# Where the left half of an output leaves from: fp16 tiles and the GpSimd queue in place of fp32 tiles and the sync queue

## The chip, the cores and the metric

The kernel runs on one core of a Trainium2 chip. The metric is device time in microseconds. The engines named below are PE (TensorE), DVE (VectorE), ACT (ScalarE), POOL (GpSimd) and SP (SyncE). POOL and SP compute little or nothing in the part that matters here: they issue DMAs.

## The reference

A dilated sliding-window attention feeds a layer of "soft MoE" slots. Only the end of the second part is touched by the change.

```python
def _moe_ref(x, phi, w1, w2):            # x: attention output, 4608 x 512
    logits = x @ phi                     # 4608 x 32
    d = softmax(logits over rows)        # dispatch
    slot_input = (d.T @ x).reshape(8, 4, 512)
    for e in range(8):
        h = np.maximum(slot_input[e] @ w1[e], 0.0)   # 4 x 1024
        slot_out[e] = h @ w2[e]                      # 4 x 512
    slot_out = slot_out.reshape(32, 512)
    c = softmax(logits over slots)       # combine
    return (c @ slot_out).astype(np.float32)         # 4608 x 512, 9.44 MB
```

Every one of the 4608 output rows depends on all of `slot_out`, so no output can be stored before the second weight matrix of all eight experts has been read.

## The kernel before

The first 137 us of the program are the attention, the logits and the slot inputs. All inputs are read by DMAs that POOL issues and that cast fp32 in HBM to fp16 on chip. The last of these are the second weights `w2`. The last two experts, 6 and 7 (`HALVED`), are loaded as column halves: first the left 256 columns of both, then the right 256 columns (`load_w2(e, half)`, L232).

The rest is an order written out by hand under `manual_schedule`: each engine runs its instructions in the order of the program text.

- `slot_out(half, experts)` multiplies the hidden rows by `w2` for one column half (PE, L681). After the last expert of a half, ACT copies that half of `slot_out` to SBUF as `so_sb` (L689).
- `combine(half, pair)` makes 256 rows by 256 columns of the output: two matmuls (L697) into a PSUM tile `f`, of which there are four, then a scaled copy to an SBUF tile `ot0` (left half) or `ot1` (right half), by ACT in two instructions for an even pair (L709) and by DVE in one for an odd pair (L713), and one DMA to `out` (L719). Left halves are fp32 tiles stored by SP; there are six buffers for the eight of them. Right halves are fp16 tiles stored by POOL, with a cast to fp32 on the way, and have eight buffers.
- `combine_full(pair)` makes 256 whole rows: one matmul for each 128 rows (L730), the first evicted by ACT (L732) and the second by DVE (L736) into one fp16 tile `of` of seven buffers, and one casting DMA by POOL (L743).

The order around the change is this:

```python
        slot_out(0, HALVED)
        at = {5: 0}
        for pair in range(NSPLIT // 2):          # 8 left halves, pairs 0 to 7
            combine(0, pair)
            if pair in at:
                slot_out(1, (HALVED[at[pair]],))  # expert 6, right columns
        slot_out(1, HALVED[1:])                   # expert 7, right columns
        for pair in range(NSPLIT // 2, NFIN // 2):
            combine_full(pair)                    # pairs 8 to 17, whole rows
            if pair >= NFIN // 2 - NSPLIT // 2:
                combine(1, pair - (NFIN // 2 - NSPLIT // 2))
```

So the left halves of the first eight pairs are made while the last right-hand weights are still arriving; then come whole rows, and from pair 10 on each is followed by the right half of an early pair.

Each DMA on POOL's queue signals one of eight semaphores in turn, and its issue waits until the DMA eight places before it has landed.

Of the kernel before, what the change touches and what calls it, by code (L numbers as in the profile page):

```python
# [9 lines left out]
FP32 = mybir.dt.float32  # L10
FP16 = mybir.dt.float16
# [13 lines left out]
DMODEL = H * D  # L25
# [18 lines left out]
NH = DMODEL // 2  # L44
NSPLIT = 16
# [25 lines left out]
def kernel(  # L71
# [10 lines left out]
    nc = tc.nc  # L82
# [534 lines left out]
    out_pool = tc.alloc_tile_pool(name="outp", bufs=1)  # L617
# [75 lines left out]
    def combine(half, pair):  # L693
        fp = psum_f.tile([128, 2, NH], FP32, name=f"f{half}_{pair}", tag="f")
        r0 = 256 * pair
        for k in range(2):
            nc.tensor.matmul(  # L697
                fp[:, k, :],
                ET[:, r0 + 128 * k : r0 + 128 * k + 128],
                so_sb[:, NH * half : NH * half + NH],  # L700
                start=True,
                stop=True,
                skip_group_check=True,
            )
        ot = out_pool.tile([128, 2, NH], (FP32, FP16)[half], name=f"ot{half}_{pair}", tag=f"ot{half}", bufs=6 + 2 * half)
        if pair % 2 == 0:
            for k in range(2):
                blk = 2 * pair + k
                nc.scalar.activation(  # L709
                    out=ot[:, k, :], in_=fp[:, k, :], func=AF.Copy, scale=rrow[:, blk : blk + 1]  # L710
                )
        else:
            nc.vector.tensor_tensor(  # L713
                out=ot,
                in0=fp,
                in1=rrow[:, 2 * pair : 2 * pair + 2, None].broadcast_to([128, 2, NH]),
                op=ALU.mult,
            )
        (nc.sync, nc.gpsimd)[half].dma_start(  # L719
            out=out[r0 : r0 + 256, NH * half : NH * half + NH].rearrange("(k p) n -> p k n", k=2),  # L720
            in_=ot,
        )

    def combine_full(pair):
        r0 = 256 * pair
        ot = out_pool.tile([128, 2, DMODEL], FP16, name=f"of_{pair}", tag="of", bufs=7)
        for k in range(2):
            blk = 2 * pair + k
            fp = psum_f.tile([128, DMODEL], FP32, name=f"f_{blk}", tag="f")
            nc.tensor.matmul(fp, ET[:, 128 * blk : 128 * blk + 128], so_sb, start=True, stop=True)  # L730
            if k == 0:
                nc.scalar.activation(  # L732
                    out=ot[:, k, :], in_=fp, func=AF.Copy, scale=rrow[:, blk : blk + 1]
                )
            else:
                nc.vector.tensor_scalar(  # L736
                    out=ot[:, k, :],
                    in0=fp,
                    scalar1=rrow[:, blk : blk + 1],
                    scalar2=None,  # L740
                    op0=ALU.mult,
                )
        nc.gpsimd.dma_start(  # L743
            out=out[r0 : r0 + 256, :].rearrange("(k p) n -> p k n", k=2), in_=ot
        )

    with tc.manual_schedule(engines=None):
        slot_out(0, ORDER[:6])
        slot_out(1, ORDER[:6])
        slot_out(0, HALVED)  # L750
        at = {5: 0}
        for pair in range(NSPLIT // 2):
            combine(0, pair)
            if pair in at:
                slot_out(1, (HALVED[at[pair]],))
        slot_out(1, HALVED[1:])
        for pair in range(NSPLIT // 2, NFIN // 2):
            combine_full(pair)
            if pair >= NFIN // 2 - NSPLIT // 2:
                combine(1, pair - (NFIN // 2 - NSPLIT // 2))  # L760
# [36 lines left out]
```

The softmax here doesn't subtract the row's maximum and nothing guards it: scores larger than these inputs give would overflow.

## Time and profile before

| | us |
|---|---|
| median of three runs (lowest, highest) | 185.91 (185.76, 186.13) |
| the profiled execution, its own time | 185.91 |
| its span, first to last instruction | 184.1 |
| last expert-7 matmul of the left half starts (L681) | 151.71 |
| SP issues the first left half (L719) | 154.13 |
| last `w2` lands, last right-half matmuls start (L681) | 157.15 |
| POOL issues the first whole-row tile (L743) | 161.36 |
| POOL issues its last output DMA (L719) | 174.32 |

Positions in the table are microseconds from the start of the span. The profiled execution's time is 1.8 us above its span, and it equals the median. In the views, a DMA "share" above 1 means that engines hold more than one packet at a time, and GB/s counts bytes as they are written: a weight load counts its fp16 bytes, an output store its fp32 bytes.

### The profile page before, as it was taken

The numbers are of one execution on the slowest core, as the hardware profiler recorded it, in microseconds if no ns is written. First come the engines' busy times: TensorE is split into PE (matmuls) and PEld (weight loads), VectorE is DVE, ScalarE is ACT, GpSimd is POOL, SyncE is SP. The second block draws the span as 40 slices with busy tenths as digits, with TensorE's granted clock in tenths as the row PEclk, the third lists the DMA queues.
The fourth block names the chain that finished last, engine by engine and source line by source line (L and its number), as shares of the span: only waits on it lengthen the run. The fifth ranks groups of instructions, "written<-read, shape, count | busy, mean of one in ns | idle before, by whom it ended". The sixth has DMA issues, their size and how long they took to land.

```text
span 184.1 us, 5522 instructions
## 1 busy us (share of the span) xinstructions
PE 142.3 (77%) x2448; PEld 85.5 (46%) x2448; DVE 104.8 (57%) x225; ACT 90.0 (49%) x161; POOL 75.1 (41%) x104
## 2 busy tenths in 40 slices
PE   3157989999999999999999999998782278587000
PEld 0134556466467467467467467564431144232000
DVE  2687779849849849849859754540420004399000
ACT  2053458576567676576576576551020006588000
POOL 7743654454453454453623755111111100089800
PEclk9999999999999999999999999965589556789755
DMA  5999999999999999999999999999999999999994
GB/s 88 199 204 212 202 206 208 210 207 206 214 209 203 212 210 203 213 206 206 213 207 208 209 211 216 214 215 214 214 214 212 197 196 191 319 325 405 408 410 91
DMA packets 32023, 41.00 MB, mean 223 GB/s; under 512 B 2144, under 2 KB 19680, under 8 KB 32000
## 3 DMA queue, kind: packets, MB, share of 16 engines
q0 software_dynamic: 29536, 38.44, 112.6%
q1 hardware_dynamic: 2464, 2.22, 3.7%
q8 instruction: 19, 0.31, 0.6%
q14 instruction: 4, 0.03, 0.0%
HBM read 62.18 MB, written 9.44 MB: 389 GB/s over the span
## 4 chain that ended last, share of the span: by engine, by line
DMA 42%; PE 30%; ACT 8%; issue 6%; POOL 6%; DVE 3%; POOLq 0%; DVEq 0%; ACTq 0%
DMA w<-in_moe_w_dram 27%; DMA vs<-in_v_dram 7%; DMA raw<-in_q_dram 6%; PE lg L413 5%; PE o_p L344 4%; PE sa L287 4%; ACT p L298 4%; PE sa L276 3%; PE sb L276 3%; ACT ot L709 3%; DMA out_dram<-ot 2%; PE f L730 2%; PE u L455 1%; PE rd L394 1%; PE vb L188 1%
## 5 line engine op out<-in xcount | busy, mean ns | idle before, releaser
L298 ACT ACTIVATE p<-sa 128x960 f16<-128x960 f32 (+2 forms) x24 | 21.4, 891 | 29.4 <-PE sb L287 28.6
L344 PEld LDWEIGHTS <-p 128*128 128x128 f16 (+2 forms) x544 | 19.4, 98 | 12.6 <-issue 8.6
L241 DVE STREAM_TRANSPOSE qk<-raw 128x576 uint32<-128x576 uint32 x16 | 20.0, 1251 | 5.7 <-DMA raw<-in_q_dram 4.5
L250 DVE STREAM_TRANSPOSE qk<-raw 128x320 uint32<-128x320 uint32 (+1 forms) x32 | 21.5, 675 | 0.3
L298 ACT ACTIVATE p<-sb 128x960 f16<-128x960 f32 (+2 forms) x24 | 21.2, 884 | 0.0
L287 PE MATMUL sa<-qk 32*128 32x160 f16 (+4 forms) x416 | 15.7, 212 | 4.0 <-DVE qk L241 4.0
L216 POOL COPY v<-v 32x1024 f16<-32x1024 f16 x8 | 8.3, 1034 | 24.7 <-DVE v L209 24.7
L413 PE MATMUL lg<-xTd,phi 128*128 128x288 f16 x32 | 18.3, 659 | 0.0
L287 PEld LDWEIGHTS <-qk 32*128 32x128 f16 x832 | 11.9, 96 | 13.4 <-issue 8.2
L232 POOL DMA_DIRECT2D w<-in_moe_w_dram x8 | 5.9, 742 | 28.0 <-DMA w<-in_moe_w_dram 23.6
L276 PE MATMUL sa<-masks,ident 128*128 128x480 f16 (+2 forms) x48 | 13.8, 372 | 4.5 <-DMA ident<-ident_d 3.0
L344 PE MATMUL o_p<-v,p 128*128 128x65 f16 (+1 forms) x288 | 16.2, 201 | 0.7 <-ACT v L197 0.7
L713 DVE TENSOR_TENSOR ot<-f,rrow 128x512 f32<-128x512 f32 (+1 forms) x8 | 5.5, 688 | 18.6 <-PE f L697 15.5
L276 PEld LDWEIGHTS <-ident 128*128 128x128 f16 x96 | 8.9, 102 | 15.2 <-issue 8.4
L287 PE MATMUL sb<-qk 32*128 32x160 f16 (+4 forms) x416 | 15.7, 212 | 0.0
L366 DVE TENSOR_TENSOR xp<-o_p,rc_p 128x448 f16<-128x448 f32 (+1 forms) x24 | 14.5, 602 | 0.8
L366 DVE TENSOR_TENSOR xd<-o_d,rc_d 128x448 f16<-128x448 f32 (+1 forms) x24 | 14.5, 602 | 0.8
L681 PE MATMUL so<-w,hTm 128*32 128x256 f16 x128 | 7.2, 361 | 9.3 <-DMA w<-in_moe_w_dram 8.5
L276 PE MATMUL sb<-masks,ident 128*128 128x480 f16 (+2 forms) x48 | 14.0, 372 | 0.4 <-ACT p L298 0.2
L220 POOL DMA_DIRECT2D w<-in_moe_w_dram x16 | 11.4, 713 | 6.3 <-DMA raw<-in_k_dram 2.6
L743 POOL DMA_DIRECT2D out_dram<-of x10 | 7.0, 701 | 15.1 <-ACT of L732 14.0
L188 PE MATMUL va<-vs,orders 32*128 32x256 f16 (+1 forms) x96 | 12.1, 289 | 1.0 <-ACT p L298 1.0
(86 smaller groups left out, 267.2 us busy)
## 6 DMA issues: line engine op xcount, KB each, us to landing
w<-in_moe_w_dram POOLq DMA_DIRECT2D x16, 512.0 KB, 17.0
w<-in_moe_w_dram POOLq DMA_DIRECT2D x6, 1024.0 KB, 27.9
out_dram<-of POOLq DMA_DIRECT2D x10, 512.0 KB, 5.6
vs<-in_v_dram POOLq DMA_DIRECT2D x8, 512.0 KB, 13.6
raw<-in_q_dram POOLq DMA_DIRECT2D x7, 576.0 KB, 15.7
raw<-in_k_dram POOLq DMA_DIRECT2D x7, 576.0 KB, 16.1
w<-in_moe_w_dram POOLq DMA_DIRECT2D x8, 256.0 KB, 24.0
out_dram<-ot SPq DMA_DIRECT2D x8, 256.0 KB, 4.0
```

The costliest lines, as they stand in the source:

```text
L188: nc.tensor.matmul(o.rearrange("p (h d) -> p h d", h=4), l, st[:, 0:4, D * r : D * r + D], start=(r == 0), stop=(r == DIL - 1), skip_group ...
L216: nc.gpsimd.tensor_copy(out=vL[b % NV][0:32, :, :, 0:D], in_=vD[b % NV][96:128, :, :, 0:D])
L220: nc.gpsimd.dma_start(out=w1t[e][:, 2 * i : 2 * i + 2, :], in_=src[:, 2 * i : 2 * i + 2, :])
L241: nc.vector.transpose(out=dst, in_=src)
L250: nc.vector.transpose(out=o, in_=i)
L276: nc.tensor.matmul(sps[h // 2][:, h % 2, 0:n], ident, bias[g], start=True, stop=False, skip_group_check=True,)
L287: nc.tensor.matmul(sps[h // 2][:, h % 2, c0 : c0 + w], kt_[32 * h : 32 * h + 32, k0 : k0 + 128, tt], qt_[32 * h : 32 * h + 32, q0 : q0 + w ...
L298: nc.scalar.activation(out=pt, in_=sps[ab][:, :, 0:n], func=AF.Exp, scale=SCALE)
L344: nc.tensor.matmul(o[p0 : p0 + np_, n, :], l, rr, start=(k == 0), stop=(k == len(jobs) - 1), skip_group_check=True,)
L366: nc.vector.tensor_tensor(out=x.rearrange("p t (h d) -> p (t h) d", h=4)[0:nq, u0:u1, :], in0=o[0:nq, 0:n, 0:D], in1=rc[0:nq, 0:n, None].b ...
L413: nc.tensor.matmul(lp, phi4[:, kc].rearrange("p c s -> p (c s)"), rhs, start=(kc == 0), stop=(kc == 3))
L681: nc.tensor.matmul(so[half][32 * a : 32 * a + 32, :], hTm[2 * g + c // 4][:, c % 4, 32 * j : 32 * j + 32], w2t[e][:, c, NH * half : NH * h ...
```

## The change

Three edits. The left-half tile `ot0` becomes fp16 with eight buffers in place of fp32 with six (`NSPLIT // 2` is 8; `ot1` already had eight). The left-half store goes by POOL's queue in place of SP's, and casts to fp32 on the way. The whole-row tile `of` has eight buffers in place of seven, for ten tiles. The order of right halves between whole rows is the same in both versions.

```diff
-        ot = out_pool.tile([128, 2, NH], (FP32, FP16)[half], name=f"ot{half}_{pair}", tag=f"ot{half}", bufs=6 + 2 * half)
+        ot = out_pool.tile([128, 2, NH], FP16, name=f"ot{half}_{pair}", tag=f"ot{half}", bufs=NSPLIT // 2)
...
-        (nc.sync, nc.gpsimd)[half].dma_start(
+        nc.gpsimd.dma_start(
             out=out[r0 : r0 + 256, NH * half : NH * half + NH].rearrange("(k p) n -> p k n", k=2),
             in_=ot,
         )
...
     def combine_full(pair):
-        ot = out_pool.tile([128, 2, DMODEL], FP16, name=f"of_{pair}", tag="of", bufs=7)
+        ot = out_pool.tile([128, 2, DMODEL], FP16, name=f"of_{pair}", tag="of", bufs=8)
```

The instructions of PE, DVE and ACT are the same in both, in the same order; eight DMA issues move from SP to POOL, ahead of POOL's first L743.

## The prediction, made before the changed kernel was run

> **What bounds the kernel now.** I read the slices of the span first: the DMA engines are busy from start to end.
>
> ```profile
> DMA  5999999999999999999999999999999999999994
> GB/s 88 199 204 212 202 206 208 210 207 206 214 209 203 212 210 203 213 206 206 213 207 208 209 211 216 214 215 214 214 214 212 197 196 191 319 325 405 408 410 91
> ```
>
> About 200 is a full rate while inputs come in (fp16 bytes counted, twice as many read); about 408 is the full rate of outputs. So this is a DMA-bound kernel, and only slices 34 and 35 (156 to 166 us) fall short: 319 and 325 of 408. The change can gain only there. I cut that stretch by events; the last two columns are DMA share and GB/s.
>
> ```profile
> 155.25:158.25 3.00, 1.59 (x21) 0.73 (x21) 0.69 (x1) 0.91 (x4) 0.00 (x0) 0.94 1.03 326
> 158.25:158.50 0.25, 0.00 (x0) 0.00 (x0) 0.00 (x0) 0.25 (x2) 0.00 (x0) 1.00 0.21 74
> 158.50:161.50 3.00, 2.50 (x6) 0.86 (x6) 2.04 (x3) 1.99 (x5) 0.14 (x1) 0.58 1.03 346
> 161.50:162.50 1.00, 1.00 (x5) 0.58 (x4) 0.90 (x2) 0.83 (x2) 0.86 (x2) 0.55 0.22 74
> 162.50:162.75 0.25, 0.25 (x4) 0.13 (x2) 0.00 (x1) 0.25 (x2) 0.25 (x1) 1.00 0.55 172
> 162.75:171.00 8.25, 5.69 (x27) 2.26 (x24) 7.44 (x11) 6.83 (x14) 8.13 (x13) 1.00 1.59 409
> ```
>
> SP's fp32 stores move 326 to 346 GB/s, then there is a hole of a full microsecond before POOL's casting stores begin, and those run at 409 to the end (180.6). Why is there a hole? The chain of waits and the list of waits say what was late:
>
> ```profile
> 154.13 3.60 DMA out_dram<-ot
> ...
> 157.84 0.84 ACT ot L709 x2
> 158.68 0.27 ACT so_sb L689
> ...
> 159.00 2.72 PE f L730 x6
> ```
>
> ```profile
> DVE ot L713 <- DMA out_dram<-ot: 3.0, 1, 3.0
> ACT ot L709 <- DMA out_dram<-ot: 2.1, 1, 2.1
> ```
>
> The seventh left tile needs the buffer of the first, whose store has to land. ACT is held 2.1 us, and behind it in ACT's order stands the copy of the right half of `so_sb`, without which no whole row can start. The timeline has the queues:
>
> ```profile
> 154.13 6.00 SPq L719 DMA_DIRECT2D out_dram<-ot  x8
> 157.15 0.29 PE L681 MATMUL so<-w,hTm 128*32 128x256 f16 x4 [0.60 <-DMA w<-in_moe_w_dram]
> 161.36 2.38 POOL L743 DMA_DIRECT2D out_dram<-of  x3 [14.02 <-ACT of L732]
> 163.73 0.71 POOL L719 DMA_DIRECT2D out_dram<-ot  x1
> ```
>
> POOL sits idle for 14 us before 161.36, so its queue has room.
>
> **What the Trainium skill says.** "DMA: Bandwidth & Descriptors", section "SWDGE vs HWDGE vs iDMA": a cast during a DMA can only be issued from GpSimd. The trace agrees as far as it goes: all fp16-to-fp32 stores are POOL's. The same page, "Latency and other measured facts", gives a first byte after about 0.6 us on the sync path and 1 us on the GpSimd path; here SP's first issue (154.13) to the first stores (155.0, where the rate jumps) is 0.9 us, POOL's (161.36 to 162.55) 1.2 us, and I use the trace. The same page, "Queues, rings and completion order": each DMA engine takes descriptors of one ring in order and alternates between rings, so on an engine that still has weights left, a POOL store stands behind them where an SP store did not. "SBUF — State Buffer", "SBUF: two separate sides": some DVE modes lock GpSimd out while it writes descriptors. The trace shows no such effect: the POOL issues of L719 and L743 take 0.70 to 0.71 us each while DVE writes fp16 tiles from PSUM, and that is the DVE form the left halves take on.
>
> **The change, part by part.** Positions are in the profiled execution, whose own time (185.91, span 184.1) is the median of the runs, so differences carry over unscaled.
>
> 1. Evictions in fp16 instead of fp32: L709 takes 0.42 us either way (2.49/6 in fp32, 0.84/2 in fp16), L713 0.69 and 0.68. Nothing, either way.
>
> 2. Eight buffers for eight left tiles. Matmuls of pairs 6 and 7 ended at about 156.3, so ACT evicts pair 6 by about 157.1 instead of 158.68. Next late is the last weight: PE's last four matmuls start at 157.15 and take 0.29. The `so_sb` copy then starts at 157.5 instead of 158.57, 1.07 us earlier, and L730 and the evictions with it. Tile `of_8` was complete at 160.86 (DVE 160.04 plus 0.82); now 159.8. DVE's 3.0 us wait goes too; nothing but its own L736 stood behind it.
>
> 3. Eight issues leave SP, where nothing stands behind them, and enter POOL ahead of L743. Price 0.71 us each, the row of the right halves, which have the same form. The first is ready when ACT ends at 154.12. A POOL issue that finds POOL asleep starts about 0.5 us after its data (160.86 to 161.36), so 154.6; the following tiles are done at 154.4, 155.0, 155.2, 155.8, 156.0, 157.1, 157.1, faster than 0.71 apart, so POOL runs without a pause: 154.6 + 8 x 0.71 = 160.3. Each issue also waits for the DMA eight places earlier. For the first six those are weights that PE has used by 155.3; for the last two (due 158.9 and 159.6) they are the last weights, landed by 157.15. For `of_8` it is the first left half. None binds. So `of_8` is issued at 160.3, 1.06 earlier than 161.36; parts 2 and 3 give the same answer, POOL setting it by a hair. Bounds: no wake-up pause gives 160.0 (data ready 159.8 plus a little), a gain of 1.4; 0.74 us each, the price of the weights' issue, gives 160.5, a gain of 0.8.
>
> 4. The DMA engines. First left half on the wire at 154.6 + 1.2 = 155.8. One is 262 kB of fp32, 0.64 us at 409 GB/s, less than the 0.71 between issues, so all eight are through by about 161.5, when `of_8` arrives (160.3 + 1.2): the hole closes and nothing piles up. From there the rest is 7.34 MB at 409 GB/s, 17.95 us, ending at 179.5 against 180.6 now. The saved SBUF reads (fp16 instead of fp32) are worth nothing by themselves[...].
>
> 5. Laggards. Between 153 and 155 the DMA share drops from 1.46 to 0.7 with nothing but weights under way: some engines finish weights long before others, and the trace's last weight packet starts at 156.7. Such an engine begins its part of the left halves 0.9 us after 155.8. It wins back 0.07 us per tile (0.71 less 0.64), 0.5 in all, and enters the whole rows 0.3 late at worst. I take off 0.1.
>
> 6. `of` with eight buffers instead of seven: no wait of L732 or L736 on a store is in the list, because the DMAs that would free them are long done. Zero; if evictions ran ahead it could only help. The right halves stand between whole rows before and after; nothing.
>
> Sum: -1.06 + 0.1, about -0.95, to **184.95 us**. About 0.2% (0.37 us) is what a measurement of this kernel can tell from no change.
>
> **Rivals.** (B) *More of the hole is won.* If POOL starts without its pause and the last weights land sooner, since SP's stores no longer share their engines, `of_8` leaves at 159.8 and the end moves by 1.6: 184.3. Against it, POOL's two limits meet at 160. (C) *The gain is hidden by one slow DMA engine.* If the engine that is last with the weights wins nothing back and also falls behind through the stores, the end is its end: 156.7 plus 9.44 MB/409 (23.1 us) plus a few tenths, some 180.3, 0.3 earlier: 185.6. For it, the two-sided share drop; against it, the final stores stop within half a microsecond of each other. (D) *Slower: POOL becomes the bound.* The eight issues must be over early enough. If each costs more than 0.71 + (161.36 - 160.3)/8 = 0.84 us, `of_8` leaves later than now, and with the left halves drained the DMA engines wait for POOL. If each paid the 0.5 us pause as the first does, they would take 9.7 us, `of_8` would leave at 163.8 to 164.3 and the time be 188.6; at half that pause, 0.96 us, 186.9. Against it: once tiles are waiting, the trace has eleven POOL issues in a row (163.73 to 171.4) 0.70 apart. That the change does not do what it says is no rival for the stores; for the right halves it is simply so.
>
> **How the numbers follow.** Forecast 0.62; B 0.14; C 0.12, split between a small gain and none; D 0.12. Faster by over 0.2%: 0.62 + 0.14 + 0.04 = 0.80; within: 0.09; slower: 0.11. The range goes from 184.1 (B's end and a little) to 186.1, which takes in C and the mild end of D.
>
> **What would show it.** Right: no wait of ACT or DVE on `out_dram<-ot`; the `so_sb` copy near 157.5; POOL L719 from 154.6, eight in a row, first L743 at 160 to 160.5; no second with a rate under 300 between 157 and 180; last stores about 179.6. Wrong: gaps between POOL's left-half issues (D), a rate well below 369 GB/s (262 kB per 0.71 us) in 157 to 161, or a few engines still storing after the others have stopped (C). The argument fails at its root if POOL's issues wait for the last weights.

## The result, and the profile after

| | before | changed |
|---|---|---|
| median, us | 186.02 (4 runs, 185.76 to 186.38) | 183.96 (4 runs, 183.67 to 184.20) |
| ratio | | 0.9887, 95% interval 0.9865 to 0.9910 |
| profiled execution, us; its span | 185.91; 184.1 | 183.95; 181.9 |

The change makes the kernel faster by 2.06 us, 1.1%. I had forecast 0.95 us and a range that ended at 184.1, so the direction was right and the size was half of what came. A second comparison of the two kernels gave 0.9891 (0.9864 to 0.9917).

The slices of the changed kernel's span: slices 34 and 35 (counted from 0; 154.6 to 163.7 us here, 156.5 to 165.7 before), which stood at 319 and 325, are now at 334 and 403. The first slice with 400 or more begins at 159.2 us instead of 165.7.

```profile
DMA  4999999999999999999999999999999999999995
GB/s 74 191 207 214 200 212 202 212 210 202 213 210 205 209 211 202 214 209 205 210 210 203 211 212 212 218 211 217 215 213 215 200 196 169 334 403 410 406 409 140
```

Stretches of the changed kernel; the last two columns are DMA share and GB/s:

```profile
155.25:157.00 1.75, 1.74 (x16) 0.75 (x13) 0.93 (x2) 0.86 (x3) 1.75 (x4) 0.50 1.78 343
157.00:160.50 3.50, 2.85 (x12) 1.17 (x13) 2.44 (x5) 3.00 (x7) 3.50 (x6) 0.97 1.91 386
160.50:161.00 0.50, 0.38 (x2) 0.10 (x1) 0.50 (x2) 0.50 (x2) 0.50 (x2) 1.00 1.75 381
161.00:171.00 10.00, 5.08 (x23) 2.11 (x22) 6.68 (x10) 6.02 (x13) 8.55 (x13) 0.99 1.60 410
...
178.50:179.00 0.50, 0.00 (x0) 0.00 (x0) 0.00 (x0) 0.00 (x0) 0.00 (x0) 0.50 1.23 248
179.00:179.50 0.50, 0.00 (x0) 0.00 (x0) 0.00 (x0) 0.00 (x0) 0.00 (x0) 0.50 0.27 55
179.50:180.00 0.50, 0.00 (x0) 0.00 (x0) 0.00 (x0) 0.00 (x0) 0.00 (x0) 0.50 0.12 25
```

The hole is gone: 386 GB/s runs into 410 without a break. But look at the last two lines. 25 GB/s is a sixteenth of 410, and 55 about two sixteenths: in the last microsecond it looks as if only one or two of the 16 DMA engines still store.

The trace lets one measure this. It keeps 16 landing times for each DMA, which I read as one for each DMA engine. The last of the 16 minus the eighth is called the *lag* below: how far the latest engine is behind the bulk. For the last tile stored, the lag is 0.29 us before and 1.22 us in the changed kernel.

The timeline of the changed kernel, line for line against the four of before:

```profile
153.91 5.61 POOL L719 DMA_DIRECT2D out_dram<-ot  x8 [7.04 <-ACT ot L709]
...
157.04 0.37 ACT L689 CAST so_sb<-so 128x256 f16<-128x256 f32 x1 [0.26 <-PE so L681]
...
159.52 2.10 POOL L743 DMA_DIRECT2D out_dram<-of  x3
...
161.60 0.71 POOL L719 DMA_DIRECT2D out_dram<-ot  x1
```

Eight issues in 5.61 us, 0.70 each, without a pause; the first whole row leaves at 159.52 instead of 161.36. In the list of waits no line of ACT or DVE on `out_dram<-ot` is left, and the chain of waits no longer holds a store. It goes through PE's own work to the copy of `so_sb` and from there to the whole rows:

```profile
152.10 2.72 PE f L697 x12
...
156.33 0.68 PE so L681 x6
157.01 0.02 issue
157.04 0.38 ACT so_sb L689
157.42 0.04 issue
157.46 0.39 PE f L730
```

Then there is the end of the program, which I had not looked at. SP waits for the last stores to land and then for the other engines. First what SP waited for, in the kernel before, then in the changed one (total, times, longest):

```profile
SPq L792 <- DMA out_dram<-ot: 21.1, 2, 17.6
SPq L792 <- PEq L792: 2.2, 2, 1.7
```

```profile
SPq L792 <- DMA out_dram<-ot: 178.9, 1, 178.9
SPq L792 <- PEq L792: 0.9, 2, 0.5
```

The longest closing wait shrank from 1.7 to 0.5 us. The view names PE, but PE had long been done; the closing instructions (line L792), of before and then of the changed kernel, show who was late. A DRAIN is one of these closing instructions; the three figures are the shortest, middle and longest of its kind in ns:

```profile
L792 POOLq DRAIN  x3: 51/98/9061, 174.3 to 183.9; - x3
L792 SPq DRAIN  x3: 7/7/7, 181.8 to 183.6; - x3
```

```profile
L792 POOLq DRAIN  x3: 51/91/7855, 173.3 to 181.6; - x3
L792 SPq DRAIN  x3: 7/7/7, 180.8 to 181.4; - x3
```

POOL's first DRAIN is the longest: it begins with POOL's last DMA issue (174.3) and takes 9061 ns, so it ends at 183.4, while SP had seen every store land by 181.8: 1.55 us in which everybody waits for POOL. In the changed kernel it ends at 173.3 + 7.86 = 181.1, 0.23 us after SP. By the trace's records the last store packet starts at 180.85 before and 179.97 after, a gain of 0.9 us; from there to the end of POOL's drain it is 2.51 and 1.16 us, a gain of 1.35. That is the difference of the spans but for a few hundredths, and more than half of it lies in a place where nothing is computed or stored.

### The profile page after: what moved, and what is told of

It is laid out like the page before. It is cut to its first block, busy times and chain, and to the rows that moved or that the text cites. A ratio compares the mean times of both kernels' runs of the same rounds, so it can differ in the third digit from the quotient of the medians.

```text
span 181.9 us, 5521 instructions
## 1 busy us (share of the span) xinstructions
PE 144.2 (79%) x2448; PEld 85.8 (47%) x2448; DVE 104.1 (57%) x225; ACT 90.2 (50%) x161; POOL 80.9 (44%) x112
## 3 DMA queue, kind: packets, MB, share of 16 engines
q0 software_dynamic: 31712, 40.54, 119.8%
## 4 chain that ended last, share of the span: by engine, by line
DMA 38%; PE 33%; POOL 8%; ACT 7%; issue 7%; DVE 3%; POOLq 1%
DMA w<-in_moe_w_dram 27%; DMA raw<-in_q_dram 6%; PE lg L413 5%; DMA vs<-in_v_dram 5%; ACT p L298 5%; PE sa L287 4%; PE o_p L344 4%; PE sb L276 4%; PE sa L276 3%; PE f L697 2%; PE rd L394 2%; PE u L455 2%; POOL out_dram L719 1%; ACT of L732 1%; PE vb L188 1%
## 5 line engine op out<-in xcount | busy, mean ns | idle before, releaser
L287 PEld LDWEIGHTS <-qk 32*128 32x128 f16 x832 | 12.6, 100 | 14.9 <-issue 9.6
L287 PE MATMUL sa<-qk 32*128 32x160 f16 (+4 forms) x416 | 16.2, 217 | 4.1 <-DVE qk L241 4.1
L276 PE MATMUL sa<-masks,ident 128*128 128x480 f16 (+2 forms) x48 | 15.0, 401 | 4.4 <-DMA ident<-ident_d 3.1
L276 PEld LDWEIGHTS <-ident 128*128 128x128 f16 x96 | 9.5, 109 | 15.8 <-issue 8.7
L287 PE MATMUL sb<-qk 32*128 32x160 f16 (+4 forms) x416 | 16.3, 217 | 0.0
L276 PE MATMUL sb<-masks,ident 128*128 128x480 f16 (+2 forms) x48 | 15.2, 403 | 0.5 <-ACT p L298 0.5
L719 POOL DMA_DIRECT2D out_dram<-ot x16 | 11.3, 710 | 7.0 <-ACT ot L709 7.0
L417 ACT ACTIVATE ET<-lg 128x288 f16<-128x288 f32 x16 | 6.6, 411 | 11.6 <-PE lg L413 11.4
L713 DVE TENSOR_TENSOR ot<-f,rrow 128x512 f16<-128x512 f32 x8 | 5.5, 688 | 11.5 <-PE f L697 11.4
```

The lines of the kernel that those rows point to most:

```text
L276: nc.tensor.matmul(sps[h // 2][:, h % 2, 0:n], ident, bias[g], start=True, stop=False, skip_group_check=True,)
L287: nc.tensor.matmul(sps[h // 2][:, h % 2, c0 : c0 + w], kt_[32 * h : 32 * h + 32, k0 : k0 + 128, tt], qt_[32 * h : 32 * h + 32, q0 : q0 + w ...
L719: nc.gpsimd.dma_start(out=out[r0 : r0 + 256, NH * half : NH * half + NH].rearrange("(k p) n -> p k n", k=2), in_=ot,)
```

## The experiments

**The same two kernels once more**, to tell chance from change. No edit.

> The kernel before, unchanged, for a second profile. Theory 1 (all of the gain is that stores start earlier and the hole near 162 us closes): the positions of its first profile come back within a few tenths of a us, and what lies between the last store and the end of the span is a constant, 3.2 us from the last packet's start. Theory 2 (part of the gain is at the very end, where POOL's closing drain ended 1.95 us after the last landing in the first profile of before and 0.64 us after it in the changed kernel): the drain again ends about 2 us after the last landing. If instead the drain is chance, it lands anywhere between 0.6 and 2 us. The last left-half expert-7 matmuls were 0.48 us earlier in the changed kernel; if that is chance, this run scatters around 151.5 too.

> The changed kernel, unchanged, for a second profile. Theory 1: last packet near 180, one DMA engine alone at the end or not, and 3 us from there to the end as before. Theory 2: POOL's closing drain again ends 0.6 us after the last landing, and one DMA engine again stores alone for the last microsecond (it stopped 1.1 us after the others in the first profile).

Before: span 184.3, last store packet 180.98, drain 2.51 us after it. Changed: span 181.8, last packet 179.88, drain 1.16 us after it. The last packets come back to 0.13 us, the drains to 0.01. The left half's copy of `so_sb` began at 152.16, 152.14 (before) and 151.68, 152.10 (changed), so that the 0.48 us of the first profile were chance, and the second profile of the changed kernel, with POOL's left halves from 154.13 and the first L743 at 159.80, is the one to hold against the forecast. A third profile of it, taken beside the last experiments, belongs here too:

> The changed kernel again, beside the other two on the same chip: ratio 0.9887 as measured, last store packet near 179.9, the drain 0.23 us after SP's.

Last packet 179.80, drain 1.17 us after it, ratio 0.9891; the first L743 is issued at 160.19.

**The buffers alone.**

```diff
-        ot = out_pool.tile([128, 2, NH], (FP32, FP16)[half], ..., bufs=6 + 2 * half)
+        ot = out_pool.tile([128, 2, NH], (FP32, FP16)[half], ..., bufs=8 - half)
```

> Left halves stay fp32 and on SP, but have eight buffers (right halves seven, to make room). Theory 1: the so_sb copy moves from 158.6 to 157.5, POOL is free, the first L743 moves from 161.4 to about 160.3, the hole closes; 1.0 us faster (ratio 0.9945), half or more of what the whole change gave. Theory 2: the data end moves by about 1 us at most and the closing drain stays as in the kernel before, about 2 us after the last landing, so 0.9 us faster at best, and the other 1.2 us of the change come only with the software queue. A rival to both: SP's stores, not the buffers, hold the stretch; then the ratio is 1.000.

Ratio 0.9973 (0.9958 to 0.9987), 0.5 us: half of what both theories expected. The first L743 is at 160.09 and the hole is closed, as I had reckoned, and the bulk of the stores (the eighth landing of the last tile) stops about 1 us sooner than before: 180.11 instead of 181.09. But the latest engine stays 0.90 us behind. Stretches of this kernel:

```profile
157.00:162.00 5.00, 3.75 (x19) 1.56 (x19) 3.28 (x6) 3.83 (x9) 1.91 (x3) 1.00 1.04 346
162.00:171.00 9.00, 4.84 (x23) 1.99 (x21) 6.36 (x10) 5.70 (x12) 7.93 (x12) 1.00 1.58 411
...
179.50:180.00 0.50, 0.00 (x0) 0.00 (x0) 0.00 (x0) 0.00 (x0) 0.00 (x0) 0.50 0.72 141
180.00:180.50 0.50, 0.00 (x0) 0.00 (x0) 0.00 (x0) 0.00 (x0) 0.00 (x0) 0.50 0.29 57
```

The last packet is at 180.52, only 0.3 to 0.5 earlier than in the two profiles of before, and the drain ends 1.55 us after SP's: the long form.

**The queue alone**, with the old numbers of buffers.

```diff
-        ot = out_pool.tile([128, 2, NH], (FP32, FP16)[half], ..., bufs=6 + 2 * half)
+        ot = out_pool.tile([128, 2, NH], FP16, ..., bufs=6 + 2 * half)
...
-        (nc.sync, nc.gpsimd)[half].dma_start(
+        nc.gpsimd.dma_start(
```

> Left halves in fp16 by POOL, but with six buffers, and of with seven. ACT and DVE wait again for the first left halves to land; these are issued at 153.9 and, behind the weights on the late engine, land near 157.5. Theory 1: so_sb near 158.2 instead of 157.0, first L743 near 161 instead of 159.5, a hole of half a us again: 0.7 us faster than before. Theory 2: the same data end, but the closing drain short as in the changed kernel, so 1.5 to 2 us faster (ratio 0.990).

Ratio 0.9936 (0.9916 to 0.9956), 1.2 us, between the two expectations. The waits for buffers are back, and so are the holes; stretches:

```profile
159.50:160.00 0.50, 0.50 (x3) 0.15 (x1) 0.18 (x1) 0.50 (x1) 0.50 (x1) 0.50 0.48 94
160.00:161.50 1.50, 1.50 (x6) 0.59 (x5) 1.32 (x2) 1.17 (x3) 0.56 (x2) 0.50 1.75 354
161.50:162.50 1.00, 1.00 (x4) 0.43 (x3) 0.75 (x1) 0.83 (x3) 0.86 (x2) 0.50 0.17 49
...
180.00:180.50 0.50, 0.00 (x0) 0.00 (x0) 0.00 (x0) 0.00 (x0) 0.00 (x0) 0.50 1.35 260
180.50:181.00 0.50, 0.00 (x0) 0.00 (x0) 0.00 (x0) 0.00 (x0) 0.00 (x0) 0.50 0.03 4
```

The first L743 is at 161.10 and the last packet at 180.54, but the drain is short (0.23 us after SP's). Together the two halves of the change give 0.9973 x 0.9936 = 0.9909, at the edge of the interval of the whole (0.9865 to 0.9910). The eighth buffer of `of` was not tested apart; no list of waits, before or after, has ACT or DVE waiting on a store of `of`.

The landings show what the hole does to the late engine (lags in us):

| kernel | hole | first left half | eighth left half | first whole-row tile | last tile |
|---|---|---|---|---|---|
| before (2 profiles) | yes | 1.43, 2.05 | 0.88, 0.63 | 0.08, 0.07 | 0.29, 0.27 |
| queue alone | yes, two | 1.19 | 0.18 | 0.09 | 0.24 |
| buffers alone | no | 2.16 | 1.19 | 0.91 | 0.90 |
| changed (3 profiles) | no | 1.57, 1.22, 1.37 | 1.27, 0.95, 1.11 | 1.30, 0.86, 0.43 | 1.22, 0.85, 0.40 |

An engine that is late with the weights catches up where the others run out of work, and keeps most of its lag where they don't. (In the third profile of the changed kernel POOL paused 0.6 us before the first whole row, and the lag fell to 0.43.) So a microsecond of hole is not worth a microsecond.

**What lengthens the drain: SP's stores, or POOL's own program?** Four single runs with a profile each.

```diff
 # no_left_stores, from before: the left halves are computed and never stored
-        (nc.sync, nc.gpsimd)[half].dma_start(
+        if half == 1: nc.gpsimd.dma_start(
 # one_on_sp, from the changed kernel: pair 0's left half in fp32, by SP
+        by_sp = half == 0 and pair == 0
-        nc.gpsimd.dma_start(
+        (nc.sync if by_sp else nc.gpsimd).dma_start(
 # act_queue, from before
-        (nc.sync, nc.gpsimd)[half].dma_start(
+        (nc.scalar, nc.gpsimd)[half].dma_start(
 # rows_in_two, from the changed kernel: each whole-row tile by two DMAs of 128 rows
-        nc.gpsimd.dma_start(out=out[r0 : r0 + 256, :]..., in_=ot)
+        for k in range(2):
+            nc.gpsimd.dma_start(out=out[r0 + 128 * k : r0 + 128 * k + 128, :], in_=ot[:, k, :])
```

> The kernel before with the eight left-half stores left out (the left halves are computed and dropped), so POOL's program is that of before to the letter and SP stores nothing. In the profiles so far POOL's closing drain ends 2.5 us after the last store packet where SP stores left halves (before twice, buffers_only) and 1.15 us after it where POOL does (changed kernel twice, queue_only). If the SP stores cause the longer drain, it is 1.15 us here; if POOL's own program does (18 output DMAs instead of 26), it is 2.5 us. Theory 1 (a constant tail) is already ruled out.

> The changed kernel, but the first left half is fp32 and stored by SP; the other seven by POOL. If any output store on SP's queue brings the longer drain, it ends 2.5 us after the last store packet; if the drain grows with the number of SP stores, 1.15 plus an eighth of 1.35, so 1.3 us; if POOL's program decides (25 output DMAs), near 1.15 us.

> The kernel before, with the left halves stored in fp32 from ACT's queue in place of SP's. If a store from any hardware queue, or POOL's own shorter program, brings the longer drain, it ends 2.5 us after the last store packet; if it is SP alone, 1.15 us. The rest as before, but ACT pays for eight issues between evictions, so the first L743 is no earlier than 161.4.

> The changed kernel, but each whole-row tile is stored by two POOL DMAs of 128 rows each, so POOL issues 36 output DMAs instead of 26, and none is on SP. If the drain depends on what SP stores, it stays at 1.15 us after the last store packet; if on POOL's count of DMAs, it moves. The stores themselves: 36 issues at 0.7 us end near 180, so POOL may become the bound, which shows as gaps and a rate under 400 GB/s after 165.

Without any store from SP (`no_left_stores`) the drain is still long; its L792 is L793:

```profile
L793 POOLq DRAIN  x3: 51/91/8981, 172.6 to 182.1; - x3
L793 SPq DRAIN  x3: 7/7/7, 180.0 to 181.9; - x3
```

172.6 + 8.98 = 181.6, 1.54 us after SP. With one store on SP it is short (0.25), from ACT's queue long (1.55), with 36 POOL DMAs 0.40. So it is not SP, but something in what POOL itself has issued. Two by-products: `no_left_stores` takes 184.1 us although 2.1 MB are never written, because its whole rows, first issued at 159.63, need their 18 us as ever (last packet 179.10), and the long drain follows. `act_queue` takes 188.53: ACT spends 0.9 to 1.55 us on two issues after each even tile, and the copy of `so_sb` slips to 161.2.

**Number of DMAs, or number of descriptors?** The kernel before, with eight unused loads on POOL in the prologue, tiny or with as many runs as an output tile; and the changed kernel with half of the left tiles on SP. Descriptors are counted by the packets of the trace: a stored half tile has 256 of 1 KB and 16 of 4 bytes, 272 in all.

```diff
 # plus8_small; plus8_full has tiles of [128, 2, 32] from 256 rows of 32 elements
+    extra = [consts.tile([16, 2], FP16, name=f"extra{i}") for i in range(8)]
...
+        for i in range(8):
+            nc.gpsimd.dma_start(out=extra[i], in_=k[0, 0, 0:16, 0:2])
 # four_on_sp, as one_on_sp but
-        by_sp = half == 0 and pair == 0
+        by_sp = half == 0 and pair < 4
```

> The kernel before with eight tiny extra loads (16 rows of two elements, not used) on POOL's queue in the prologue; the outputs are issued exactly as in before. POOL's closing drain, counted from SP's last drain, ended 1.55 us after it with 18 output DMAs on POOL (before, buffers_only, no_left_stores, act_queue) and 0.23 to 0.40 us after it with 25, 26 and 36. If the drain depends on how many DMAs POOL has issued in the whole program (where its ring of descriptors stands), it is short here too, and the kernel is up to 1.3 us faster than before, less what the eight issues cost early (5.7 us of POOL, which is mostly idle there). If it depends on what POOL issues at the end, or on the bytes or descriptors of it, it stays at 1.55 us and the time is that of before or a little over.

> As the run with eight tiny loads, but each extra load has 128 partitions of two short runs, so as many descriptors as a stored left half. If the drain follows the number of descriptors issued in the whole program, it is short here (0.25 us after SP's last drain) even where the tiny loads leave it at 1.55; if only the end of POOL's program matters, 1.55 us in both. Some us slower than before through the many short runs.

> The changed kernel, but the first four left halves are fp32 and stored by SP, the other four by POOL (22 output DMAs on POOL). It places the step of the drain between 18 and 25: 1.55 or 0.25 us after SP's last drain, or something between. The stores: SP's four start at 155.0 without standing behind the weights, POOL's four follow, no hole; first L743 near 159, the bulk of the stores ends within 0.3 us of the changed kernel's 178.8. If the late engine's lag comes from standing behind weights in POOL's ring, it is a few tenths smaller here (last packet 179.5). With the short drain 183.6, with the long one 184.9.

Both `plus8` kernels are 4 us slower (189.93, ratio 1.0211, 1.0168 to 1.0254; and 190.52), a miss: each extra issue waits for the DMA eight places earlier, so the next load of `q` leaves at 24.4 us instead of 11.0. Their ends answer the question nevertheless. First the tiny loads, then the full ones:

```profile
SPq L795 <- PEq L795: 2.2, 2, 1.7
```

```profile
SPq L795 <- PEq L795: 0.9, 2, 0.5
```

The same number of DMAs, the same outputs at the end, SP's stores as in before: the drain is long (1.55 us after SP's) with 29792 packets in POOL's queue and short (0.24) with 31712, which is the changed kernel's number. With four left halves on SP (30624 packets) it ends together with SP's.

**Only the descriptors of before changed** (four whole-row tiles as two DMAs each, so four DMAs more), and the time measured.

```diff
-        nc.gpsimd.dma_start(out=out[r0 : r0 + 256, :]..., in_=ot)
+        for c in range(0, DMODEL, NH if pair < 12 else DMODEL):
+            w = NH if pair < 12 else DMODEL
+            nc.gpsimd.dma_start(out=out[r0 : r0 + 256, c : c + w]..., in_=ot[:, :, c : c + w])
```

> The kernel before, with the whole-row tiles of pairs 8 to 11 each stored by two POOL DMAs of 256 columns instead of one of 512. SP keeps the left halves, buffers and evictions are those of before; POOL's ring gets 4 x 272 = 1088 more packets, 30624 in all, as many as with four left halves on POOL. If POOL's closing drain follows the number of descriptors in its ring (1.55 us after SP's last drain at 29536 and 29792 packets, 0.0 at 30624, 0.23 to 0.40 from 31440 up), it is hidden behind SP's here, and the kernel is 1.1 to 1.5 us faster than before although its stores move no earlier: ratio 0.993. If what counts is that left halves are stored by POOL, the drain stays at 1.55 us and the ratio is 1.000 to 1.002.

Ratio 0.9961 (0.9944 to 0.9979): 0.7 us faster, with the left halves still on SP, the same buffers, and the last store packet 0.6 us later than in the first profile of before (181.46; the split rows run at 362 to 389 GB/s, which is close to the 374 that one issue of 262 kB every 0.70 us allows). The drain is no longer seen at all:

```profile
L794 POOLq DRAIN  x3: 51/97/7580, 174.9 to 183.1; - x3
L794 SPq DRAIN  x3: 7/7/7, 182.6 to 182.9; - x3
```

It ends at 182.5, before SP. The gain is below the 1.1 to 1.5 us expected by what the stores lost. All profiles together, with times counted from SP's first closing drain:

| packets in POOL's queue | kernels | POOL's drain ends after SP's, us |
|---|---|---|
| 29536 | before (2), buffers_only, no_left_stores, act_queue | 1.54 to 1.55 |
| 29792 | plus8_small | 1.55 |
| 30624 | four_on_sp (2), before_split4 | -0.01, -0.14 |
| 31440 | one_on_sp | 0.25 |
| 31712 | changed (3), queue_only, plus8_full | 0.23 to 0.24 |
| 31872 | rows_in_two | 0.40 |

**A better version?** Four left halves on SP came out at 183.52 us, ratio 0.9862 (0.9821 to 0.9902), so I ran it beside the changed kernel.

> Four left halves on SP and four on POOL, again, beside the changed kernel on the same chip. In the first profile its last store packet was 0.5 us earlier (179.4 instead of 179.9) and the drain wholly hidden, span 0.65 us shorter. If that holds, its time is 0.3 to 0.7 us under the changed kernel's (ratio to before 0.9855 against 0.9887); if the first profile was luck, they are the same.

0.9877 (0.9854 to 0.9901) against the changed kernel's 0.9891 in the same comparison: the intervals overlap and the medians are 0.2 us apart. It hides the drain, but its last packet was at 179.40 and 179.85 in two profiles; it is not shown to be better.

## Why the prediction was right and wrong

- *The buffer wait, part 2: right.* The copy of `so_sb` moved to 157.04, 157.46 and 157.43 in three profiles (forecast 157.5). In the last two the weights were next, as said: PE waited 0.37 us for them. In the first they had landed at 156.54, and PE's own work came last.
- *POOL's issues, part 3: right in kind, a little pessimistic.* Eight in a row, none waiting for weights. The sleep ahead of the first was 0.28 us rather than 0.5 (ACT ends at 153.63, POOL starts at 153.91), and each took 0.70. The first L743 came at 159.52, 159.80 and 160.19, against 160.3.
- *The DMA engines, part 4: right for the bulk.* The hole closed, and the eighth landing of the last tile came at 179.25 to 179.91 instead of 181.09 and 181.26. The gain is 1.2 to 2.0 us, more than the 1.06 of the forecast. That type and queue of a tile cost nothing was assumed and is not shown: SP's fp32 halves landed 0.76 us apart with the buffers alone, POOL's fp16 halves 0.70, and POOL's queue and fp16 were never changed apart.
- *The laggards, part 5: mis-sized.* I had the late engine start its part of the left halves 0.9 us late, win back 0.5 and enter the whole rows 0.3 late at worst. The lag at the first left half was 1.2 to 1.6 us. The bulk landed one half every 0.70 us, which is POOL's pace of issue, and the late engine one every 0.66, so it won back 0.3 in all and entered the whole rows 1.30, 0.86 and 0.43 us late. I had taken off 0.1 us. The late engine ate what parts 3 and 4 gave beyond the forecast: the last packet moved from 180.92 (mean of two) to 179.88 (mean of three), 1.0 us, against my 0.95. For the stores the right number came from two errors that cancelled, which is luck. Rival C named this mechanism, but allowed it a gain of 0.3 us only. That a POOL store suffers more than an SP store by standing behind the weights is not borne out: with SP's stores the lag at the first left half was 1.4 to 2.2 us.
- *The sum: the step that failed.* It ended with the last store ("179.5 against 180.6 now") and carried the difference over to the time, as though everything after it were the same. It is not: POOL's closing drain gave another 1.35 us. I priced a DMA that moves to POOL's queue by its issue alone. The view with the clue was at hand, SP's closing wait of 1.7 us and the 9061 ns DRAIN in the kernel before. No rival had it. On the other side, the time around the span grew from 1.76 to about 2.0 us (1.90 to 2.06 in three profiles); 1.0 + 1.35 - 0.25 is the 2.1 us measured. Why the time around the span grew is open: it was 1.96 and 2.05 in `rows_in_two` and `one_on_sp`, and 1.75 to 1.79 in the other eleven profiles, the queue alone among them.

What the runs show of the drain is that it follows what was put into POOL's queue over the whole program, and not SP's stores, the number of DMAs or the outputs at the end. Counted from the last store packet it ends 2.45 to 2.51 us later up to 29792 packets, 0.98 to 1.04 later at 30624, and then 1.13 to 1.23 from 31440 to 31872. Why it falls and then rises a little is open: that the place where the count of packets ends matters, and not how many they are, would fit, but it was not tested apart, and the exact place of the step is not known.

## What to carry to other kernels

Read the last instructions of the profile as you read the loop: compare the ends of the engines' closing drains, and if one engine alone is late, that time is part of what is measured and can move when DMAs change queue or shape. In a DMA-bound end, look at the last microsecond engine by engine; a hole lets late DMA engines catch up, so closing it is worth less than its length. Where a sum ends at the last store, say what follows it and why that should stay the same.

## What I had not expected of the hardware

POOL's closing DRAIN ended 1.55 us after SP had seen the last store, or within 0.4 us of it, depending on the packets that POOL had issued since the start. For a given program this came back to 0.01 us (1.55 in two profiles of before, 0.23 in three of the changed kernel).

The DMA engines don't run in step: the 16 landings of the last weights lie 3.4 to 4.4 us apart in before and the changed kernel (153.17 to 156.54 in its first profile), and the late engine carried up to 1.2 us of that through the more than 20 us of stores that followed. Only where the bulk ran out of work did the lag fall to 0.1 us.

SP's fp32 stores with runs of 1 KB moved 346 GB/s at a DMA share of 1.04; POOL's casting stores of the same runs moved 386 at a share of 1.91, at POOL's pace of one issue every 0.70 us, and 410 with runs of 2 KB mixed in.
